# A deep cross network on one core: first loads over two DMA queues, bias rows transposed by TensorE, a layer's weights queued ahead of the combinations before it, and own order lists for the first eight units

## The chip, the cores and the metric

The kernel runs on one core of one Trainium2 chip. The metric is the device time of one execution in microseconds (us). A profiled execution has a span about 2 us shorter than its device time.

Engines are named as in the profile: PE is TensorE's matmuls, PEld its weight loads, DVE is VectorE, ACT is ScalarE, POOL is GpSimd, SP is SyncE. SPq, ACTq and POOLq are DMAs that these engines issue.

## The reference

Six layers of a deep cross network on a batch of 16384 rows of 1024 bf16 numbers:

```python
def reference(x0, ws, bs):            # (16384, 1024), (6, 1024, 1024), (6, 1024), all bf16
    x = x0
    for l in range(ws.shape[0]):
        proj = jnp.einsum('bd,de->be', x, ws[l]) + bs[l]
        x = x0 * proj + x
    return x
```

## The kernel before

The kernel works on pairs of 512-row blocks, 16 pairs of 6 layers, 96 "units". Each unit is a fast matrix product in Winograd's form: the weight matrix of a layer is cut in four quadrants (1, 12, 2, 4), four sums of quadrants (5, 6, 7, 3) are made by VectorE, and 7 quadrant products (P1 to P7, each 16 matmuls of 512 columns) take the place of 8. Units of the first pair and the last unit use one level; the others split products 5 and 2 once more ("two-level"), for which VectorE also makes the inner combinations 2i and 5i. Every combination made in the first pair is stored to a DRAM buffer `Lc` and loaded again by the later pairs. The input of a unit is cut in quarters too: q00 is needed by P1, q10 by P2, q01 (through T1 = q01 - q00) by P5, and q11 (through T2 = q11 - T1) by P6.

The order of all instructions on all engines is fixed when the program is built: each operation has a rank, and a heap emits them by rank. Every engine then works strictly in that order.

```python
R0 = ranks(""" ... c5@-8.6 c6@-6.8 c7@-4.5 c3@11.9 2i7@-7.4 2i5@-7.1 2i6@.5 ...""")   # one-level units
RFIRST = {**R0, **ranks("T1@-5 c5@-4.5 T2@-4 c6@-3.5 ... 2i5@15 2i6@15.1 ...")}     # first unit
...
isum = [work.tile([P, KH, H], BF16, name=f"isum{i}") for i in range(2)]    # buffers of 2i and 5i
...
for u, (pr, l) in enumerate(units):                  # order in which weight tiles are taken
    if pr == 0:
        ring_seq += [(u, w, k) for w, k in (("1", "load"), ("2", "load"), ("w12", "stage"), ("4", "load"),
                                            ("5", "make"), ("6", "make"), ("7", "make"), ("3", "make"))]
...
def combo(name, w, a, b, o_, deps, u=u, raw=raw):    # a sum of quadrants, and its store to Lc
    def fn():
        t = ring_make(u, w)
        tt(t[:], raw(a)[:], raw(b)[:], o_)
        nc.gpsimd.dma_start(Lc[units[u][1], CIDX[w]].rearrange("p (k e) -> p k e", k=KH), t[:])
    ...
combo("c5", "5", "w12", "4", ADD, ())
combo("c6", "6", "5", "1", SUB, ("5",))
...
for i in range(NDUMMY):                              # 24 dummies, to bring TensorE's clock up
    nc.tensor.matmul((pX + pA)[i % (2 * KH)][:], lhsT=zeros[:, 0:P], rhs=zeros[:], ...)
...
load_quarter(0, 0); take(1)                          # q00 (DMA transpose), w1
load_quarter(1, 0); take(1)                          # q10, w2
load_quarter(0, 1); take(2)                          # q01, w12, w4
load_quarter(1, 1)                                   # q11: all on the Sync queue
nc.sync.dma_start_transpose(out=b_bf[:], in_=bs.rearrange("l (m p) -> (l m) p", p=P))
nc.gpsimd.tensor_copy(b_all[:], b_bf[:])
```

## Time and profile before

| | before |
|---|---|
| device time, median of 4 | 2287.74 us (2287.15 to 2288.21) |
| PE busy | 99% of the span |
| first useful matmul | 9.2 us |
| start of P6 in the first layer | 25.7 us |
| start of the third layer | 67.0 us |

The last two rows are read from the trace by counting weight loads without the dummies: P6 is the 49th, the third layer the 225th (a one-level layer has 112). Between the two lie 176 matmuls, which take 38.0 us at 0.216 us each. Before, 41.25 us passed, so 3.3 us were lost on that way.

The head of the profile page, with the busy time of the engines and the chain of waits:

```profile
span 2285.3 us, 34998 instructions
PE 2270.2 (99%) x12960; PEld 1265.4 (55%) x12960; DVE 2080.7 (91%) x2324; ACT 1837.7 (80%) x3228; POOL 20.8 (1%) x43
PE 97%; DVE 1%; SPq 1%; DMA 1%; ACT 0%; issue 0%; DVEq 0%
```

The kernel is bound by TensorE nearly everywhere, so what can be won without cheaper matmuls lies mostly in the start. Who TensorE waited for in the first 250 us, the dummies left out (total us, times, longest us):

```profile
PE pX L204 <- ACT ev L213: 4.7, 1, 4.7
PE pX L204 <- DVE xst L118: 3.1, 1, 3.1
PE pX L302 <- DVE ti L118: 0.6, 2, 0.4
```

The timeline shows where the first two are (start us, duration us, engine, line, operation, out<-in; in brackets the idle time before it and what ended it). Of the tile names, `wp` is a weight quadrant or a sum of them, `w` the quadrant w12, `x0T` the input, `T` the combinations T1 to T4, `pX` and `pA` the PSUM banks that matmuls write, `ev` what is read out of these, `xst` a layer's output, `isum` the inner combinations 2i and 5i, `ti` the input combinations of two-level products:

```profile
12.40 4.45 SPq L440 DMA_TRANSPOSE x0T<-in_x_dram  x1
...
16.90 1.22 SPq L457 DMA_TRANSPOSE b_bf<-in_bs_dram  x1
17.10 1.23 DVE L118 TENSOR_TENSOR wp<-w,wp 128x2048 bf16<-128x2048 bf16 x1 [2.52 <-DMA wp<-in_ws_dram]
18.16 1.13 SPq L165 DMA_DIRECT2D wp<-in_ws_dram  x2
...
18.96 1.22 DVE L118 TENSOR_TENSOR T<-x0T,T 128x2048 bf16<-128x2048 bf16 x1 [0.64 <-DMA x0T<-in_x_dram]
...
19.89 3.27 SPq L165 DMA_DIRECT2D wp<-in_ws_dram  x3
...
20.30 2.42 ACT L213 ACTIVATE ev<-pX,b_all 128x512 bf16<-128x512 f32 x4 [6.27 <-POOL b_all L458]
21.04 5.06 PE L204 MATMUL pX<-T,wp 128*128 128x512 bf16 x16 [4.70 <-ACT ev L213]
...
34.36 1.23 DVE L118 TENSOR_TENSOR wp<-w,wp 128x2048 bf16<-128x2048 bf16 x1 [4.49 <-DMA wp<-in_ws_dram]
...
46.47 1.89 PE L204 MATMUL pX<-xst,wp 128*128 128x512 bf16 x8 [3.10 <-DVE xst L118]
```

The line at 17.10 is c5, which waited for w4. The one at 18.96 is T2, which waited for q11. At 20.30 the first bias activation starts at last: the bias transpose was issued behind everything else. P5 follows at 21.04, first at half clock: 7 of its matmuls start 0.427 us apart. At 34.36 the second layer's c5 starts, for whose weights VectorE stood 4.49 us, and TensorE pays at 46.47.

### The profile page before, as it was taken

How to read it: one execution, taken by the hardware profiler on the slowest of the kernel's cores; microseconds unless marked ns; L12 is line 12 of the kernel's file. 1: busy time of each engine (PE TensorE's matmuls, PEld its weight loads, DVE VectorE, ACT ScalarE, POOL GpSimd, SP SyncE). 2: the span in 40 equal slices, each digit the busy share in tenths (PEclk: the TensorE clock that was granted, in tenths of full speed). 3: DMA queues.
4: the chain of work that ended last, by engine and by line, in shares of the span. 5: the costliest groups of instructions: out<-in, count | busy, mean ns of one | idle time of the engine just before them, and what ended most of it. 6: DMA issues, size and time to landing. Idle time of an engine off the chain costs nothing.

```text
span 2285.3 us, 34998 instructions
## 1 busy us (share of the span) xinstructions
PE 2270.2 (99%) x12960; PEld 1265.4 (55%) x12960; DVE 2080.7 (91%) x2324; ACT 1837.7 (80%) x3228; POOL 20.8 (1%) x43
## 2 busy tenths in 40 slices
PE   8999999999999999999999999999999999999999
PEld 3445555555555555555555555555555555555554
DVE  6999999999999999999999999999999999999997
ACT  4668788888888888888878888888888888888887
POOL 1100000000000000000000000000000000000000
PEclk9999999999999999999999999999999999999999
DMA  9669689695986959779697796977969789596872
GB/s 296 239 242 290 229 235 282 195 313 193 255 270 205 311 192 252 261 218 302 210 252 258 222 285 216 260 252 224 291 203 273 243 227 289 196 295 223 238 244 68
DMA packets 624828, 557.01 MB, mean 244 GB/s; under 512 B 397584, under 2 KB 551184, under 8 KB 624656
## 3 DMA queue, kind: packets, MB, share of 16 engines
q1 hardware_dynamic: 618944, 535.64, 78.7%
q0 software_dynamic: 5184, 18.88, 2.1%
q8 instruction: 101, 1.65, 0.3%
q14 instruction: 71, 0.58, 0.1%
q10 hardware_dynamic: 528, 0.26, 0.0%
HBM read 436.21 MB, written 52.43 MB: 214 GB/s over the span
## 4 chain that ended last, share of the span: by engine, by line
PE 97%; DVE 1%; SPq 1%; DMA 1%; ACT 0%; issue 0%; DVEq 0%
PE pA L204 57%; PE pX L302 24%; PE pX L204 16%; DVE ev L118 1%; DMA wp<-in_ws_dram 1%; SPq L440 1%; DVE xst L118 0%; ACT ev L213 0%; DVE T L118 0%; DVE wp L118 0%; SPq L447 0%; SPq L165 0%; DVE isum L118 0%; SPq L457 0%; DVE x0T L400 0%
## 5 line engine op out<-in xcount | busy, mean ns | idle before, releaser
L204 PEld LDWEIGHTS <-wp 128*128 128x128 bf16 x7904 | 772.6, 98 | 849.9 <-issue 7.0
L204 PE MATMUL pA<-T,wp 128*128 128x512 bf16 x4608 | 1056.9, 379 | 0.1
L213 ACT ACTIVATE ev<-pA,b_all 128x512 bf16<-128x512 f32 x1124 | 706.0, 689 | 212.3 <-PE pA L204 212.3
L302 PEld LDWEIGHTS <-wp 128*128 128x128 bf16 x4984 | 487.1, 98 | 158.2 <-issue 16.9
L118 DVE TENSOR_TENSOR ev<-ev,x0T 128x2048 bf16<-128x2048 bf16 (+2 forms) x484 | 483.4, 1000 | 7.8 <-ACT ev L213 1.3
L118 DVE TENSOR_TENSOR xst<-ev,xst 128x2048 bf16<-128x2048 bf16 x319 | 389.0, 1220 | 19.4 <-DVE ev L118 0.5
L302 PE MATMUL pX<-ti,wp 128*128 128x256 bf16 x2848 | 398.1, 272 | 0.6 <-DVE ti L118 0.6
L118 DVE TENSOR_TENSOR ev<-ev,ev 128x2048 bf16<-128x2048 bf16 (+1 forms) x283 | 343.9, 1215 | 28.2 <-ACT ev L213 11.3
L213 ACT ACTIVATE ev<-pX,b_all 128x512 bf16<-128x512 f32 x412 | 289.1, 705 | 66.2 <-PE pX L204 49.3
L204 PE MATMUL pX<-xst,wp 128*128 128x512 bf16 x1376 | 337.7, 379 | 3.1 <-DVE xst L118 3.1
L204 PE MATMUL pA<-xst,wp 128*128 128x512 bf16 x1280 | 313.5, 379 | 0.0
L209 ACT COPY pX<-pA 128x512 f32<-128x512 f32 x412 | 256.5, 627 | 60.3 <-PE pA L204 60.2
L209 ACT CAST ev<-pX 128x512 bf16<-128x512 f32 x384 | 224.7, 619 | 39.2 <-ACT ev L213 38.0
L118 DVE TENSOR_TENSOR ev<-iu,ip 128x1024 bf16<-128x1024 bf16 x178 | 122.5, 688 | 121.0 <-ACT iu L209 121.0
L209 ACT COPY pX<-pX 128x512 f32<-128x512 f32 x356 | 208.9, 587 | 8.5
L209 ACT CAST iu<-pX 128x512 bf16<-128x512 f32 x356 | 196.8, 639 | 0.3 <-PE pX L302 0.2
L118 DVE TENSOR_TENSOR T<-xst 128x2048 bf16<-128x2048 bf16 x160 | 195.0, 1218 | 0.5
L118 DVE TENSOR_TENSOR T<-xst,T 128x2048 bf16<-128x2048 bf16 x160 | 195.1, 1219 | 0.4
L302 PE MATMUL pX<-T,wp 128*128 128x256 bf16 x1068 | 160.2, 273 | 0.0
L209 ACT CAST ip<-pX 128x512 bf16<-128x512 f32 x178 | 104.8, 589 | 55.0 <-PE pX L302 55.0
L302 PE MATMUL pX<-xst,wp 128*128 128x256 bf16 x888 | 133.2, 273 | 0.0
L118 DVE TENSOR_TENSOR xst<-ev,x0T 128x2048 bf16<-128x2048 bf16 x64 | 78.2, 1224 | 1.6
(41 smaller groups left out, 628.5 us busy)
## 6 DMA issues: line engine op xcount, KB each, us to landing
wp<-Lc SPq DMA_DIRECT2D x538, 512.0 KB, 4.5
wp<-in_ws_dram SPq DMA_DIRECT2D x288, 512.0 KB, 5.3
out_dram<-x0T SPq DMA_DIRECT2D x30, 1024.0 KB, 9.9
Lc<-wp POOLq DMA_DIRECT2D x24, 512.0 KB, 6.1
Lc<-isum POOLq DMA_DIRECT2D x12, 512.0 KB, 3.6
w<-in_ws_dram SPq DMA_DIRECT2D x6, 512.0 KB, 7.4
out_dram<-x0T SPq DMA_DIRECT2D x2, 512.0 KB, 3.4
out_dram<-x0T SPq DMA_DIRECT2D x3, 256.0 KB, 2.9
```

Of the source, the lines that this page charges most:

```text
L118: nc.vector.tensor_tensor(out=o, in0=a, in1=b, op=op)
L204: nc.tensor.matmul(bank[:], lhsT=wt[(u, w)][:, k, m * P:(m + 1) * P], rhs=rhs[:, k, :], start=(start and k == 0), stop=(k == KH - 1), skip ...
L209: add(name, lambda: nc.scalar.copy(out=dst, in_=src), rd, wr)
L213: add(name, lambda: nc.scalar.activation(out=dst, in_=src, func=IDENT, bias=b_all[:, c:c + 1], scale=1.0), rd, wr)
L302: nc.tensor.matmul(pX[bank][:, m * NQ:(m + 1) * NQ], lhsT=wv[:, k, m * P:(m + 1) * P], rhs=rhs[:, k, :], start=(start and m == 0 and k == ...
L440: nc.sync.dma_start_transpose(out=blk(x0Ts[0], dh, n), in_=x0[n * NB:(n + 1) * NB, dh * H:(dh + 1) * H])
```

## The change

Its intent: bring the first weights and activations in earlier by two queues, take the bias off the end of the Sync queue, queue the next layer's raw weights before they are wanted, and give each of the first eight units an order list of its own, with inner combinations deferred behind the critical work. The diff, cut to its core:

```diff
-RFIRST = {**R0, **ranks("T1@-5 c5@-4.5 T2@-4 c6@-3.5 ...")}
+EARLY = [ranks("P1.3@-.68 ... 2i5@-7.88 2i6@-7.41 2i3@-6.94 2i7@-6.47 c5@4.62 T1@5.76 c5b@7.12 c6@7.86 T2@9.00 ... 5i7@54.56"),
+         ranks("... 2i5@-7.12 c5@-6.28 ..."), ranks("... 2i7@-24.53 2i5@-9.30 c5@-7.83 ..."), ... ]     # eight lists
...
-    NDUMMY = 24
+    NDUMMY = 14
...
-    isum = [... for i in range(2)]
+    isum = [... for i in range(4)]            # layer l uses 2*(l % 2) and 2*(l % 2) + 1
...
+    RAW = [("1", "load"), ("2", "load"), ("4", "load"), ("w12", "stage")]
+    MAKE = [(w, "make") for w in ("5", "6", "7", "3")]
+    ring_seq = [(0, w, k) for w, k in RAW]
     for u, (pr, l) in enumerate(units):
         if pr == 0:
-            ring_seq += [(u, w, k) for w, k in (... raw loads of u, then its makes ...)]
+            ring_seq += [(u + 1, w, k) for w, k in RAW if l < L - 1] + [(u, w, k) for w, k in MAKE]
...
-        rk = RFIRST if first else (RLAST if last else (R0 if one else R2))
+        rk = EARLY[u] if u < len(EARLY) else (RLAST if last else (R0 if one else R2))
...
+            if first:                          # c5 in two halves of columns, each for two groups of P5
+                def c5a(): ...
+                def c5b(): ...
...
+    for w in ("1", "2"):
+        nc.scalar.dma_start(wt[(0, w)][:], w_src(0, w))
+    nc.scalar.dma_start(b_rows[:], bs.rearrange("l (m p) -> (l m) p", p=P))
+    load_half(nc.scalar, "w12", 0); load_half(nc.scalar, "4", 0)
     load_quarter(0, 0); load_quarter(1, 0); load_quarter(0, 1)
+    load_half(nc.sync, "w12", 1); load_half(nc.sync, "4", 1)
     load_quarter(1, 1)
-    nc.sync.dma_start_transpose(out=b_bf[:], in_=bs.rearrange("l (m p) -> (l m) p", p=P))
-    nc.gpsimd.tensor_copy(b_all[:], b_bf[:])
+    nc.tensor.matmul(pX[KH - 1][:, 0:LK], lhsT=b_rows[:], rhs=ident[0:LK, 0:LK], start=True, stop=True, ...)
+    nc.vector.tensor_copy(out=b_all[:], in_=pX[KH - 1][:, 0:LK])
```

## The prediction

> **What bounds the kernel.** TensorE: the page gives PE 99% busy over a 2285.3 us span, and the chain of waits is 97% PE. Steady matmuls of 512 columns start every 0.216 us (timeline); a one-level unit of 112 takes 24.2 us, and the change makes no matmul cheaper. Only time in which TensorE stands or runs at half rate can be won. From successive matmul starts in the timeline, against 0.216 us each:
>
> 1. Start: first useful matmul at 9.2 us, after 24 dummies (1.19 to 9.2).
> 2. First layer, before the P5 products: from 15.96 to 21.04 us nothing starts, 4.9 us lost. c5 (the w12+w4 sum) ends at 18.3, because w4 lands at 17.05. Then P5 still waits for bank readers: the first bias activation waits until 20.3 for the GpSimd bias cast, which waits 18.1 us for the bias DMA transpose, last on the Sync queue.
> 3. After that hole 7 matmuls run at 0.427 us: 1.45 us lost. The Trainium skill ("TensorE: Matmul & The Clock Gate", "What's actually happening") gives an idle window of about 3.4 us for half clock; this trace agrees: a 4.9 us hole does it.
> 4. Second layer, 42.99 us: 3.3 us lost. TensorE waits for VectorE's xst. VectorE had stood 4.5 us (to 34.36) for the second layer's weights, queued late, and is otherwise full from 43 to 150 us.
> 5. Entry to two-level units, 165 to 174 us: 1.6 us in short waits.
>
> Sum of 2 to 5: 11.2 us, half a percent.
>
> **What the change does.**
> - Bias rows: a plain small load, one TensorE transpose, one small VectorE copy; removes the 20.3 us gate. Cost: P1 now stands behind the bias landing, third on the ScalarE queue.
> - Two queues: the same 4.19 MB must arrive. In the trace q00 lands at 4.7, w1 7.4, q10 9.3, w2 11.5, q01 13.2, w12 15.2, w4 17.05, q11 18.9 us. The skill ("DMA: Bandwidth & Descriptors", "Issuing engines are not separate DMA queues") says queues share the same engines; the trace shows them already 90 to 100% busy from 2 to 18 us, so I expect only the small gaps between transfers back: all landed at about 17.5 to 18. w12 and w4 come earlier, in halves, so c5's first half releases P5.0 and P5.1.
> - 14 dummies end at about 7.1 us, when the clock turns full. I expect P1 at about 8.5 (7.5 to 9.5), P5 without a real hole, T2 at about 18, P6 at about 19.7 instead of 25.94: 6.2 us won, half-rate stretch included.
> - Weights of the next layer ahead: VectorE's 4.5 us idle goes, and with it hole 4 (3.3 us).
> - Inner combinations (about 0.42 us each, 8 per layer) deferred behind the critical chain with four isum buffers, and unit 6 interleaved: most of hole 5 (about 1.3 us). VectorE has about 25 us of work per 24.2 us unit, so deferral spills into later units, which have about 2 us free each.
> - Back: about 1 us of new short waits at the joins.
>
> Sum: about -10 us: **2278.0 us, 8 in 10 between 2275.0 and 2282.5.** Faster by over 2%: 0.01; within 2%: 0.98; slower: 0.01.
>
> **Right if** the profile shows PE holes under 1.5 us in the first 175 us, no matmuls at 0.427 after the dummies, P6 near 20 us, bias activation no later than its matmul, unit 1 starting near 33.5 us (before 39.75), and the span from there unchanged.
>
> **Wrong if** the bias rows land late and hold P1 (each us late is one us); two queues slow the first activation quarter; VectorE, in order, is blocked by an inner combination placed first; or weight tiles held by deferred combinations delay unit 6's loads.

## More of the kernel before

The four loads of the second layer were issued from 18.16 to 19.89 us, directly behind the first loads. The last, w4, was under way for 14.38 us, as the chain of waits has it (start us, us, what):

```profile
19.89 14.38 DMA wp<-in_ws_dram
```

## The result

| | before | after |
|---|---|---|
| device time, median of 4 | 2287.74 us | 2280.60 us (2279.11 to 2280.97) |
| first useful matmul | 9.2 us | 9.2 us |
| start of P6 in the first layer | 25.7 us | 21.9 us |
| lost from P6 to third layer | 3.3 us | 1.6 us |
| start of the third layer | 67.0 us | 61.5 us |

The ratio of the two is 0.9968, with a 95% interval of 0.995 to 0.9985. Ratios are the mean time of one kernel's fast runs over that of the other's of the same rounds, so not quite the ratio of the medians. The change won 7.1 us, within the 2% that count as the same and inside the predicted range. The third layer starts 5.4 us earlier; 0.4 us more come from layers three to five (0.13 us each), and the rest is the entry to the two-level units, where short waits of 1.6 us together fell to about 0.4.

The head of the page after. The trace lacks some 240 matmul records, which lowers PE's count and busy time; weight loads are complete, which is why I count those.

```profile
span 2279.1 us, 34736 instructions
PE 2252.4 (99%) x12713; PEld 1263.8 (55%) x12951; DVE 2079.8 (91%) x2326; ACT 1841.2 (81%) x3228; POOL 20.0 (1%) x42
PE 96%; DVE 1%; SPq 1%; issue 1%; DMA 1%; ACT 0%; DVEq 0%; ACTq 0%
```

TensorE's waits in the first 250 us after, the dummies again left out:

```profile
PE pX L558 <- DMA b_rows<-in_bs_dram: 3.3, 1, 3.3
PE pX L284 <- DVE T L197: 2.6, 2, 1.5
PE pX L284 <- DVE wp L197: 0.9, 1, 0.9
PE pX L396 <- DVE ti L197: 0.2, 1, 0.2
```

The bias wait of ScalarE is gone, and so is the single hole of 4.7 us. In its place stand three shorter ones, seen in the timeline after:

```profile
9.07 0.19 PE L558 MATMUL pX<-ident,b_rows 48*128 48x48 bf16 x1 [3.28 <-DMA b_rows<-in_bs_dram]
...
11.40 0.67 POOL L331 DMA_DIRECT2D Lc<-isum  x1 [10.09 <-DVE isum L197]
...
16.26 1.23 DVE L197 TENSOR_TENSOR T<-x0T 128x2048 bf16<-128x2048 bf16 x1 [4.31 <-DMA x0T<-in_x_dram]
...
17.54 1.04 PE L284 MATMUL pX<-T,wp 128*128 128x512 bf16 x3 [1.15 <-DVE T L197]
18.47 1.68 SPq L245 DMA_DIRECT2D wp<-in_ws_dram  x3
...
18.77 0.69 DVE L197 TENSOR_TENSOR wp<-w,wp 128x1024 bf16<-128x1024 bf16 x1 [1.28 <-DMA wp<-in_ws_dram]
...
19.52 2.76 PE L284 MATMUL pX<-T,wp 128*128 128x512 bf16 x12 [0.94 <-DVE wp L197]
...
20.19 0.51 SPq L245 DMA_DIRECT2D w<-in_ws_dram  x1
...
20.66 1.23 DVE L197 TENSOR_TENSOR T<-x0T,T 128x2048 bf16<-128x2048 bf16 x1
...
31.73 1.23 DVE L197 TENSOR_TENSOR wp<-w,wp 128x2048 bf16<-128x2048 bf16 x1 [2.36 <-DMA w<-in_ws_dram]
...
44.48 1.89 PE L284 MATMUL pX<-T,wp 128*128 128x512 bf16 x8 [1.48 <-DVE T L197]
```

Here q01 lands at 16.2 us (before it was 13.2: issue at 7.91 and 5.3 us to landing), c5's second half is at 18.77, and T2 starts at 20.66, 1.7 us later than before. The line at 11.40 is new in this place: VectorE makes the first layer's 2i early, and its 0.5 MB store now runs in front of q11. The wait at 19.52 comes from the new list itself: behind P5.0 it puts P5.3, which needs c5's second half, so the early half served one group and not two. The second layer's loads were issued from 18.47 to 20.19 us, again directly behind the first loads and no earlier than before, although queueing them early was an intent of the change. At 31.73 VectorE still waits 2.4 us for the second layer's w12, and TensorE pays 1.5 us at 44.48.

Why q01 and q00 are later shows in the DMA view of the stretch from 3 to 4 us after (queue, packets, MB, share of the 16 engines; q10 is the ScalarE queue, q1 the Sync queue):

```profile
q10 hardware_dynamic: 264, 0.25, 72.8%
q1 hardware_dynamic: 352, 0.09, 40.6%
```

Weights with 1 KB packets move 0.25 MB in that microsecond, transposes with 256 B packets 0.09 MB. q00 therefore took 8.2 us from issue to landing, at 8.94 us; before, alone, it took 4.0 and landed at 4.7.

### The profile page after: what moved, and what is told of

Its sections match the earlier page's. It is cut to its first block, busy times and chain, and to the rows that moved or that the text cites. A ratio compares the mean times of both kernels' runs of the same rounds, so it can differ in the third digit from the quotient of the medians.

```text
span 2279.1 us, 34736 instructions
## 1 busy us (share of the span) xinstructions
PE 2252.4 (99%) x12713; PEld 1263.8 (55%) x12951; DVE 2079.8 (91%) x2326; ACT 1841.2 (81%) x3228; POOL 20.0 (1%) x42
## 4 chain that ended last, share of the span: by engine, by line
PE 96%; DVE 1%; SPq 1%; issue 1%; DMA 1%; ACT 0%; DVEq 0%; ACTq 0%
PE pA L284 56%; PE pX L396 24%; PE pX L284 16%; DVE ev L197 1%; SPq L534 1%; DMA w<-in_ws_dram 1%; DVE xst L197 0%; ACT ev L293 0%; DVE T L197 0%; DVE isum L197 0%; SPq L547 0%; SPq L245 0%; DVE wp L197 0%; DVE x0T L494 0%; ACT pX L289 0%
## 5 line engine op out<-in xcount | busy, mean ns | idle before, releaser
L284 PE MATMUL pA<-xst,wp 128*128 128x512 bf16 x1205 | 302.3, 379 | 4.0
```

Source lines behind the costliest of these rows:

```text
L284: nc.tensor.matmul(bank[:], lhsT=wt[(u, w)][:, k, m * P:(m + 1) * P], rhs=rhs[:, k, :], start=(start and k == 0), stop=(k == KH - 1), skip ...
```

## The experiments

Four calls were made, each on one chip with the kernel before beside it; times are compared with the kernel before of the same call. The first theory (A) was that bandwidth and packet order bind the start and that two queues bring nothing; it changed as results came in. "Lost" is the loss from P6 to the third layer.

| run | median us | against before | P6 starts | lost | third layer starts |
|---|---|---|---|---|---|
| after | 2280.60 | -7.1 | 21.9 | 1.6 | 61.5 |
| r1_bias_dma | 2283.27 | -4.3 | 26.3 | 0.0 | 64.3 |
| r2_one_queue | 2282.71 | -4.9 | 24.7 | 0.0 | 62.7 |
| r4_loads_only | 2284.36 | -3.2 | 21.6 | 4.7 | 64.3 |
| r3a_prefetch1 | 2284.30 | -3.3 | 22.1 | 4.7 | 64.8 |
| r5_bias_only | 2289.64 | +1.8 | 23.6 | 6.5 | 68.1 |
| m1_store_late | 2280.77 | -7.0 | 20.3 | 3.5 | 61.8 |
| m4_raw_order | 2283.12 | -4.7 | 22.6 | 4.0 | 64.6 |
| m5_dummies24 | 2280.61 | -7.2 | 21.4 | 4.2 | 63.6 |
| d1_stores_late | 2286.28 | -2.4 | 22.1 | 7.4 | 67.5 |
| d3_before_stores | 2294.12 | +5.4 | 25.7 | 9.1 | 72.8 |
| d2_stores_isum | 2277.77 | -9.5 | 20.3 | 0.0 | 58.2 |
| d4_best | 2277.97 | -9.3 | 20.6 | 0.0 | 58.6 |

Two notes on the table. The positions are of the profiled execution; those of r4, r3a, m1, m4, m5 and d1 were the slowest of their five (m5's by 2.5 us over its median, the others' by 0.3 to 1.4). And no row's median differs from before by 2%; the differences between rows are read from the traces, and the medians mostly go the same way.

### r1_bias_dma: the changed kernel with the old bias path

```diff
-    nc.scalar.dma_start(b_rows[:], ...)
-    nc.tensor.matmul(pX[KH - 1][:, 0:LK], lhsT=b_rows[:], ...); nc.vector.tensor_copy(out=b_all[:], ...)
+    nc.sync.dma_start_transpose(out=b_bf[:], ...)          # behind q11
+    nc.gpsimd.tensor_copy(b_all[:], b_bf[:])
```

> The changed kernel with the bias rows again by a DMA transpose last on the Sync queue and a GpSimd cast. Theory A (bandwidth and packet order bind the start): in the changed kernel q00 landed at 8.94 us and the bias rows at 9.07, so P1 starts no earlier than 8.9 us without the bias in front of it; the transposed bias lands behind q11 at about 22 us, the first bias activation runs at about 23 us, P5 waits for it, the clock falls to half again, and P6 starts at 27 to 28 us instead of 21.9: 5 to 6 us longer than the changed kernel, about 2286. Rival B (the bias rows third on the ScalarE queue were what held P1): P1 starts at 7.5 us or earlier.

P1 started at 9.38, held by q00, so the bias rows on the ScalarE queue were not what held it: rival B falls. P6 came at 26.3, just short of the 27 to 28 expected, and the clock fell to half again. But the time grew by only about 2.8 us against the changed kernel, not 5 to 6. The 4.4 us that P6 lost were partly given back, because the loss from P6 to the third layer fell from 1.6 to 0.0: TensorE came late enough for VectorE to be ready. This was the first sign that the holes do not add up. (One side effect: the early 2i store stood behind the bias cast on GpSimd here and was issued only at 20.55 us.)

### r2_one_queue: first loads whole, on the Sync queue alone

```diff
-    nc.scalar: w1, w2, bias, first halves of w12 and w4     nc.sync: q00, q10, q01, second halves, q11
+    nc.scalar: bias                                         nc.sync: q00, w1, q10, w2, q01, w12, w4, q11
```

> The changed kernel with all first loads whole and on the Sync queue in the order of the kernel before (q00, w1, q10, w2, q01, w12, w4, q11); only the bias rows (12 KB) stay on the ScalarE queue. Theory A (two queues bring no bandwidth, and 1 KB weight packets crowd out 256 B transpose packets): q00 lands at 4.7 instead of 8.94, P1 starts at about 7.4 (w1), q01 lands at about 13.2 instead of 16.2, q11 at 19 to 20 instead of 20.6, P6 starts at 20.3 to 21.3 instead of 21.9, 0.5 to 1.5 us shorter than the changed kernel. Rival B (two queues are what won the time): P6 starts at 23 us or later and the time is 1 us or more longer than the changed kernel.

The start went as theory A said: q00 took 4.3 us to landing and P1's first useful matmul was at 7.7 us. P6 did not. It came at 24.7 us instead of 20.3 to 21.3, which is the rival's number, and the time was about 2.2 us longer than the changed kernel's. The timeline of this run shows why:

```profile
17.84 0.69 DVE L197 TENSOR_TENSOR wp<-w,wp 128x1024 bf16<-128x1024 bf16 x1 [4.43 <-DMA wp<-in_ws_dram]
18.45 1.22 DVE L197 TENSOR_TENSOR T<-x0T 128x2048 bf16<-128x2048 bf16 x1
...
19.73 5.31 PE L284 MATMUL pX<-T,wp 128*128 128x512 bf16 x15 [4.35 <-DVE T L197]
```

w4 is late in this order, c5's first half stands before T1 in VectorE's list, and P5 waits for both; the half clock follows. So theory A is right about bandwidth and wrong about the verdict: the two queues win no bandwidth, but they bring the first halves of w12 and w4 (landed at 9.70 and 11.16 us) in front of q01, which is where P5 needs them. Here w4 landed at 17.75, and T1 stood behind c5 although its q01 had landed at 13.5. q11 landed at 21.7, not at 19 to 20: the 2i store, issued at 13.72, stood in front of it here too. The early P1 is worth nothing here. One queue in another order (w12 and w4 ahead of q01, or T1 first in the list) was not run, so the number of queues and the order of the loads are not told apart.

### r4_loads_only and r3a_prefetch1: without the order lists

```diff
 r4_loads_only
-        rk = EARLY[u] if u < len(EARLY) else ...
+        rk = RFIRST if first else ...                       # lists of the kernel before (c5b right behind c5)
-            ring_seq += [(u + 1, w, k) for w, k in RAW if l < L - 1] + [(u, w, k) for w, k in MAKE]
+            ring_seq += [(u, w, k) for w, k in RAW if u] + [(u, w, k) for w, k in MAKE]
 r3a_prefetch1: the same lists, but the second layer's RAW ahead of the first layer's MAKE
```

> The changed kernel with the order lists of the kernel before for all units and each layer's raw weights queued behind the combinations as before: what remains is the first loads on two queues, the bias by TensorE, the halves of c5 and 14 dummies. Theory A: P6 starts at 20.5 to 21.5 (there is no early store of inner combinations before q11), but the hole of the second layer comes back at 3 us or more and the entry to the two-level units costs 1.5 us again: 2282 to 2284, 2 to 3 us longer than the changed kernel. Rival C (order lists and early weights do nothing; all the gain is in the first load): within 0.7 us of the changed kernel.

> As the run before, but the second layer's raw weights alone are queued ahead of the first layer's combinations; order lists as in the kernel before. Theory A: the second layer's weights land before VectorE asks for them, so the hole of the second layer falls from over 3 us to under 1.5; the entry to the two-level units still costs about 1.5 us. 0.5 to 1.5 us longer than the changed kernel, about 2281.5. Rival D (the new order lists close that hole, not the earlier weights): the hole stays over 2.5 us and the time is that of the run before within 0.5 us.

Without the lists, P6 starts as early as in the changed kernel (21.6), but 4.7 us are lost to the third layer, of which 3.0 are the wait for xst and the rest is half clock behind it, and the waits at the entry to the two-level units are back (1.5 us). r3a lost the same 4.7 us, the number of rival D. But its edit did not do what I meant: the second layer's loads were issued 2.7 us behind q11 in both runs (16.57 after 13.88 in r4, 17.57 after 14.87 in r3a), so nothing was queued earlier, and r3a does not test theory A against D. In these two runs VectorE did not wait for the second layer's weights by more than 0.5 us, and the loss was there all the same: with the old lists VectorE's work itself is too long for that place. The early queueing of weights can't be taken away from the changed kernel while the lists stay: the program then does not build, because the list asks for the third layer's w2 before its load is queued. So that single part was not tested.

### r5_bias_only: the kernel before with the new bias path alone

```diff
-    nc.sync.dma_start_transpose(out=b_bf[:], ...); nc.gpsimd.tensor_copy(b_all[:], b_bf[:])
+    nc.scalar.dma_start(b_rows[:], ...)                     # ahead of the first loads
+    nc.tensor.matmul(pX[KH - 1][:, 0:LK], lhsT=b_rows[:], ...); nc.vector.tensor_copy(out=b_all[:], ...)
```

> The kernel before with the new bias path alone (rows loaded first on the ScalarE queue, TensorE transpose, VectorE copy). Theory A2 (after T2, VectorE and what it waits for bind the first two layers): P5 starts at about 18.5 instead of 21.0 and P6 at about 22 instead of 25.9, but VectorE still stands until w4 of the second layer lands at about 34.3, so the hole of the second layer grows from 3.3 to about 7 us and the time falls by less than 1 us (2286.7 to 2287.6). Rival B2 (the holes add up, as the prediction summed them): the hole stays at 3.3 us and the time falls by about 4 us, to 2283.6.

P6 came 2.1 us earlier, and the kernel was not faster: its median is 1.8 us *longer*, with a ratio of 1.0006 (0.9993 to 1.002). That it is slower is not clear of the noise; the 4 us that the sum of holes promised (a ratio of 0.998) are excluded. The loss to the third layer grew from 3.3 to 6.5 us: TensorE arrived earlier at a place where VectorE was not ready, stood there 4.0 us instead of 3.3, and then ran 8 matmuls at half clock. Theory A2 is right in kind; it was wrong in saying that VectorE's chain stays where it was. VectorE now waited 3.2 us for the store of a 2i buffer, which it wants to overwrite (there are only two here). Rival B2, that the holes add up, is refuted. It was also the way my prediction had summed. (Of the 2.6 us by which the profiled execution is longer than before, 1.1 are there at the third layer; 1.3 come later than 200 us, where the edit changes nothing, and stay unexplained.)

### m1_store_late, m4_raw_order, m5_dummies24: one small thing each

```diff
 m1_store_late: the first layer's 2i is stored by an operation of its own
+                    if X == "2i":
+                        add("2isave", save, [f"2i0.{r}" for r in "5637"])       # rank 16.5, behind c3
 m4_raw_order: the second layer's raw weights are issued w12, w4, w1, w2; their places in the ring stay
 m5_dummies24
-    NDUMMY = 14
+    NDUMMY = 24
```

> The changed kernel with only the store of the first layer's w2 inner combinations issued later (behind c3), its VectorE work left where it is. Theory A: the store was 0.5 MB in front of q11 at 13.5 to 15 us; without it c5's second half and T2 come 1.2 us earlier and P6 starts at about 20.7 instead of 21.9. VectorE's wait for w12 of the second layer (until 31.7) moves by about as much, so about 1.2 us of the time is won: 2279.4. Rival (A2 strictly: only the landing of the second layer's w12 counts, and the later store holds it where it was): P6 earlier, but the hole of the second layer grows by as much, time within 0.4 us of the changed kernel.

> The changed kernel with only the order in which the second layer's raw weights are issued changed: w12 and w4 (which c5 needs first) before w1 and w2. Theory A2: w12 lands before 27 us instead of 31.7, VectorE does not stand 2.4 us for it, and the hole of the second layer (1.64 us) falls below 0.4: about 1.3 us won, 2279.3. Rival (VectorE is simply full there, the wait does not matter): hole and time unchanged within 0.4 us.

> The changed kernel with 24 dummies as before instead of 14. Theory A3 (with 14 dummies TensorE stands 2.5 to 3.6 us before P1, and in some executions the clock has fallen to half by then, as in two of the experiments so far): P1 starts where it did (9.0 to 9.4), never at 0.427 us a matmul, the median is 0.2 to 0.6 us lower and the spread under 1 us. Rival (the dummies delay P1): P1 starts later than 9.4 and the time is longer.

m1 moved T2 from 20.66 to 19.27 and P6 from 21.9 to 20.3, a little more than expected: the early store did stand in front of q11. And the time stayed (-7.0 against -7.1), because the loss to the third layer grew by as much. (The rival's number came, but not its reason: the second layer's w12 did land earlier, at 29.0 us instead of 31.6.) m4 was worse than the changed kernel by about 2.5 us. Who VectorE waited for from 19 to 50 us, first in m1, then in m4:

```profile
DVE isum L197 <- DMA wp<-in_ws_dram: 2.8, 1, 2.8
DVE wp L197 <- DMA w<-in_ws_dram: 1.1, 1, 1.1
```

```profile
DVE isum L197 <- DMA wp<-in_ws_dram: 5.1, 1, 5.1
DVE wp L197 <- DMA wp<-in_ws_dram: 1.4, 1, 1.4
```

In m4 w12 is there in time, and now an inner combination waits 5.1 us (to 34.1) for w2, which went last. In m1 the third layer's 2i7, which the new list puts far ahead (rank -24.53), waits 2.8 us for the third layer's w2. That w2 landed at 37.8 us. So when one wait is shortened, VectorE, in order, stands at the next raw weight that is late. Both "expected" numbers failed for this reason.

m5 gained nothing: P1 started at 9.6, at full clock, and the median was the same. Half clock in P1 and P2, which m4 had in 13 matmuls, was not free there: TensorE stood nowhere between P1 and P6, and P6's first matmul came 0.7 us after T2 was ready (22.84 against 22.14). m5's profiled execution had 4.2 us lost, with VectorE waiting 4.8 us for w12. The changed kernel lost 1.6 us and waited 2.4. That the landing of these weights moves from run to run would explain the spread of both kernels (1.9 and 3.4 us); this is argued, not shown.

### d1_stores_late, d3_before_stores: the first layer's stores out of the way

```diff
 def combo(...):   # first layer only: the store becomes an operation of its own
-        nc.gpsimd.dma_start(Lc[...], t[:])
+        if u > 0: put()
+    if u == 0: add(name + "s", put, [f"w0.{w}"], (), [w])
 # ranks of the five stores: just behind the second layer's c5 on the GpSimd queue
```

> The changed kernel with the five early stores of the first layer's combinations (2i, 5, 6, 7, 3) issued behind the second layer's c5 on the GpSimd queue; nothing else moved. Theory A4 (while a store with 4 KB packets is in flight, loads with 1 KB packets get about 90 KB per us instead of 350, so the second layer's raw weights land at 31.7 us, and VectorE, which works in order, waits for them): those weights land by 27 us, VectorE's wait for w12 of the second layer (2.4 us) goes, P6 starts at 20.3 to 20.8 as with the late 2i store alone, and the holes of the second layer together fall below 0.8 us: 2277.5 to 2278.5. Rival E (the weights are late because they are queued late, whatever the stores do): they land after 30 us, and the time stays within 0.5 us of the changed kernel.

> The kernel before with only the first layer's five stores (2i, 5, 6, 7, 3) issued behind the second layer's c5. Theory A4: w4 of the second layer lands by 29 us instead of 34.3, VectorE's wait of 4.5 us falls below 0.5, and the second layer's hole falls from 3.3 us to under 0.5: 3 us shorter, about 2284.7, nearly half of what the whole change won. Rival E (the load was queued too late, or VectorE's work itself is too long): the hole stays over 2.5 us and the time within 0.7 us of before.

Both missed badly: d1 was 4 to 5 us slower than the changed kernel, d3 5.4 us slower than before. The first step of theory A4 was nevertheless seen to hold, and d3 shows it most cleanly: against the kernel before only the stores were moved. The second layer's w4 was issued at 20.00 us, as before (19.89), but landed at 27.2 instead of 34.3, and c5 began without a wait:

```profile
29.90 1.22 DVE L118 TENSOR_TENSOR wp<-w,wp 128x2048 bf16<-128x2048 bf16 x1
```

In d1 the second layer's w12 landed at 26.3 us instead of 31.6. The loads ran at about 350 KB per us from 20 to 31 us, and VectorE's waits for weights between 19 and 50 us were gone. In their place stands a wait that I had made myself, first d1, then d3:

```profile
DVE isum L197 <- DMA Lc<-isum: 8.3, 1, 8.3
```

```profile
DVE isum L118 <- DMA Lc<-isum: 10.2, 1, 10.2
```

The 2i store was the last of the five, and a later layer's inner combination overwrites the buffer that it reads. In d1 that is the third layer's 2i7, placed early by the list; in d3, with two buffers, the second layer's. The whole queue of stores had to finish first. In d3 TensorE also stood 5.0 us before the second layer. The profile puts that down to a weight load, but w1 had landed at 22.0; VectorE's first `xst`, held up behind the 10.2 us, ended at 44.7, and TensorE went on at 44.84.

### d2_stores_isum, d4_best: the same, mended

```diff
 d2_stores_isum, against d1
-  ranks 2isave@18.4 c5s@18.0 c6s@18.1 c7s@18.2 c3s@18.3        third layer: 2i7@-24.53
+  ranks 2isave@17.95 c5s@18.0 c6s@18.1 c7s@18.2 c3s@18.3       third layer: 2i7@-9.25
-    NDUMMY = 14
+    NDUMMY = 24
 d4_best, against d2
-    nc.scalar: w1, w2, bias, w12/0, w4/0      nc.sync: q00, q10, q01, w12/1, w4/1, q11
+    nc.scalar: bias, w1, w2, w12, w4/0        nc.sync: q00, q10, q01, w4/1, q11
```

> The run with late stores again, mended where it made its own wait: the 2i store is the first of the five behind the second layer's c5 (it was the last, and the third layer's 2i7 waited 8.3 us to overwrite the same buffer), the third layer's 2i7 stands 15 us later in the order, and 24 dummies as before keep the clock up. Theory A4 (VectorE's waits for weights and buffers bind the second layer): no wait over 0.8 us on VectorE between 19 and 50 us, the second layer's holes together under 1 us, P6 at 20.3 to 21.3, third layer from 59.5 to 60.3 instead of 61.5, 2278.0 to 2279.5, that is 1 to 2.5 us below the changed kernel. Rival F (the pipe finds another wait; the start is bound by VectorE's amount of work): the third layer does not start before 61 us and the time is within 0.5 us of the changed kernel or longer.

> As the run before, with another split of the first loads: ScalarE queue bias, w1, w2, w12 whole and the first half of w4; Sync queue q00, q10, q01, second half of w4, q11. Fewer 512 B packets (w12 goes in 1 KB packets): q11 lands about 0.5 us earlier, at about 18.7, c5's second half no longer waits behind q01, P6 at 20.0 to 20.8: 0.3 to 0.8 us below the run before. Rival (whole w12 ahead of the transposes delays q00 and q01 as much as it saves): P1 later than 9.8 us and no gain.

d2 did what theory A4 says, and a little more: 2277.77 us (2277.2 to 2278.02), 9.5 us below before; the ratio is 0.9957 (0.9945 to 0.997). The changed kernel had won 7.1; none of its four executions was under 2279.1. P6 starts at 20.3, nothing is lost to the third layer, and the only waits of VectorE between 8 and 50 us are these:

```profile
DVE b_all L568 <- PE pX L567: 8.3, 1, 8.3
DVE T L197 <- DMA x0T<-in_x_dram: 2.7, 1, 2.7
DVE wp L197 <- DMA wp<-in_ws_dram: 1.3, 1, 1.3
DVE ev L197 <- ACT ev L293: 0.3, 1, 0.3
```

The DMA view of the stretch from 26 to 30 us tells the cause. First the kernel before, then the changed one, then d2 (q0 is the GpSimd queue with the stores, q1 the Sync queue with the loads):

```profile
q0 software_dynamic: 329, 1.22, 74.7%
q1 hardware_dynamic: 394, 0.40, 28.1%
```

```profile
q1 hardware_dynamic: 842, 0.83, 59.0%
q0 software_dynamic: 218, 0.76, 46.7%
```

```profile
q1 hardware_dynamic: 1413, 1.40, 109.8%
```

In the kernel before the stores move 1.22 MB in these 4 us and the loads 0.40, that is 100 KB per us. In d2 the loads have the engines to themselves and move 350 KB per us. The bytes in total are even fewer (1.40 MB against 1.62); what counts is which bytes come first. The three edits of d2 against d1 were not separated, and the later 2i7 and the 24 dummies were not run together without the late stores; so the traces show why the weights come early, but not how the gain in time is shared out. The dummies alone gave nothing in m5; in d1, though, P1 started at 9.9 us and ran 8 matmuls at half clock, and P6's first matmul came 1.4 us after T2 was ready (22.33 against 20.96), so once q11 is early they may count.

d4 gained nothing over d2. P1 came earlier (8.2) instead of later, then TensorE waited 1.7 us for q10. q11 landed at 18.3, 0.6 us earlier than in d2, and T2 was ready at 19.6; but P6 came at 20.6, within the expected range and no earlier than d2's 20.3, because TensorE, late from q10, had no other wait up to it. This split moved the wait from q11 to q10.

## Why the prediction was right or wrong

**The number was right.** 2280.6 us lies inside 2275.0 to 2282.5 and is "same" at 2%. The won time was 7.1 us where the text said about 10, so the point forecast was 2.6 us too low. Part of this is luck: the range took in any gain from 5.2 to 12.7 us, and two of its three terms came short (3.8 us instead of 6.2 in the first layer, 1.6 instead of 3.3 in the second). Of the prediction's own tests under "Right if", those of the clock and of the bias held, but P6 came at 21.9 instead of near 20, the second layer (its "unit 1") began at 35.9 instead of 33.5, and holes of 3.3 us (before P1) and 1.6 us (second layer) stood.

**Right: the places.** TensorE's loss was in the start, and after 250 us nothing was won. The bias gate is gone. Hole 5, at the entry to the two-level units, fell from 1.6 to about 0.4 us; r4 and r3a, with the old lists, have 1.5 us of it back, so the order lists, or the order of the weight loads that went with them, closed it.

**Wrong in size: "all landed at about 17.5 to 18".** T2 started at 20.66, when q11 had landed, and P6 at 21.9 instead of 19.7; so 3.8 us were won there and not 6.2. I had named the term, two queues sharing the same engines, but took only gaps back from it. Not even the gaps came back: without the early 2i store q11 landed at 18.9 to 19.7 us on two queues (m1, d1, d2, r1, r4, r3a; 18.3 in d4's split) and at 18.9 to 19.2 on one (before, d3, r5). The early 2i store then cost 1.4 us (T2 starts that much earlier without it, in m1). Two more things may have lengthened it: loads in halves, whose 512 B packets, with 256 B transposes among them, moved 0.26 MB in the microsecond from 16.3 us (1 KB packets moved about 0.35 in d1 and d2), and the crowding of transposes by larger packets. How much belongs to these two was not measured.

**Wrong: "VectorE's 4.5 us idle goes, and with it hole 4 (3.3 us)".** 2.4 us of the idle and 1.6 us of the loss stayed. The reason I gave, weights "queued late", was not the cause. The second layer's loads were issued at 18.2 to 19.9 us before and at 18.5 to 20.2 after, in both directly behind the first loads; but they were crowded out by the stores of the first layer's combinations. d3 shows it for the kernel before (w4 issued at the same time, landed at 27.2 instead of 34.3), d1 and d2 for the changed one (w12 at 26.3 and 26.9 instead of 31.6). With those stores out of the way, and with no buffer to wait for, both the idle and the loss fall to nothing (d2).

**Wrong: the sum.** I added the holes as if each could be closed by itself. r5 refutes this: the bias part alone moved P6 2.1 us forward and won nothing. r1, r2, d2 and d4 lose nothing between P6 and the third layer; in m1 and r5 the loss grew by as much as P6 had gained, or more. The third layer starts at the later of two times: P6 plus 38.0 us (TensorE's chain), or the time at which VectorE, in order, has got through its waits for weights and buffers. Before, after and in m1, the second was the later.

**The named risks.** "Two queues slow the first activation quarter" came true (q00 at 8.94 instead of 4.7) and cost P1 about 0.7 us against my 8.5, but r2 shows that P1's start did not matter. "The bias rows land late and hold P1" came true in the profile (3.3 us of wait), yet r1 shows q00 just behind it. "VectorE is blocked by an inner combination placed first" came true in m1, m4, d1 and d3, not in the changed kernel's own profile.

**On the skill pages.** The Trainium skill, "DMA: Bandwidth & Descriptors", section "Issuing engines are not separate DMA queues", says that DMAs of several engines run on the same 16 DMA engines. The traces agree: without the early 2i store the last first load landed at 18.9 us or later on two queues (18.3 in d4's split), and at 18.9 on one. The same page, section "Queues, rings and completion order", says that each engine goes round-robin between queues, a packet at a time; a packet is there a group of some 9 to 17 descriptors, and no run shows whether the profile's packets are the same. The traces fit turns of one profile packet each, roughly: with packets of 1 KB against 256 B, 0.25 against 0.09 MB in a microsecond; with stores of 4 KB against loads of 1 KB, 1.22 against 0.40 MB in four. I had read the first section and not drawn the consequence of the second.

## What to carry to other kernels

When an engine works in a fixed order, closing a hole in front of it can just move the hole, as in r5 and m1: compute for each chain (here TensorE's and VectorE's) when it could arrive at the next meeting point, and mend the later one first. Look at the packet sizes of what runs together in a tight stretch: a transfer that nobody waits for, with large packets, took the DMA engines from loads with small ones here (100 KB per us instead of 350), and issuing it later (d3's first store, 31.4 instead of 20.2, brought w4 7 us forward) can be worth more than issuing the load earlier. Before moving a store, check who overwrites the buffer that it reads.

## What the Trainium skill lacked or had wrong

- "DMA: Bandwidth & Descriptors", section "Queues, rings and completion order": it gives the round-robin by packets but not its price. Here two queues in contention moved bytes at about 3 to 1 where the sizes of their packets in the profile were 4 to 1: loads with 1 KB packets fell from about 350 KB per us to 100 (26 to 30 us, d2 against before) beside stores with 4 KB packets, and 256 B transposes to 90 KB beside 1 KB weight loads.
- The same page, section "Issuing engines are not separate DMA queues", says that a second queue only saves issue time. It also changes who comes first: q00 landed at 8.94 us instead of 4.7 when weights moved to a second queue, and the first halves of w12 and w4 came early enough to let P5 start at 17.54 us, against 19.73 with one queue (r2_one_queue).
- "TensorE: Matmul & The Clock Gate", section "What's actually happening": half clock after at least one idle window of about 3.4 us. Less than a whole window was enough: in r4_loads_only a wait of 2.6 us before P1 was followed by 7 matmuls at half clock, while the changed kernel's wait of 3.3 us was followed by none. In each of the 14 traces the clock changes of the first 50 us lie whole multiples of 3.41 us apart (r4: 5.50, 8.92, 12.33, 43.05, 46.46). Counted in windows of this grid, TensorE stood 2.6 us within one window in r4, but 1.9 and 1.6 us in two neighbours in the changed kernel. All 16 windows in which it stood 2.2 us or more were followed by half clock; of those with less, one brought the clock down (d1, 2.0 us).
- No page that I read says that a buffer's store makes the next writer wait as a load does: a queue of five 0.5 MB stores held VectorE 8.3 and 10.2 us in d1 and d3.
